# Reading shared rows through several copies in DRAM: roots of a norm in four transfers, rows of decays stored eight times

## The chip, the cores and the metric

The kernel runs on one core of a Trainium2 chip. The metric is the device time of one execution in microseconds. One execution was also taken by the hardware profiler; its page and trace give the start and end of every instruction and DMA. The engines are PE (matmuls; PEld is its weight load), DVE (vector), ACT (scalar, activation functions), POOL (GpSimd) and SP, which here only issues DMAs.

## What is computed

The reference is a state-space layer (Mamba-2 in chunks) with 4 sequences of 8 heads and 768 steps, followed by a feed-forward layer with a gate on its 3072 tokens of width 256:

```python
# batch 4, heads 8, seq 768, head_dim 32, d_state 16
cum = np.cumsum(log_a in the chunk)
L = exp(cum[:, None] - cum[None, :]) * causal          # decays inside a chunk
y = ((C @ B.T) * L) @ x + (C @ state) * exp(cum)       # inside the chunk + from the state
state = exp(sum(la)) * state + sum_j B_j x_j exp(cum_end - cum_j)
...
xn = x / sqrt(mean(x * x) + 1e-6) * rms_g              # x: (3072, 256)
g, val = xn @ w_gate, xn @ w_val                       # 256 -> 1536
out = (g * sigmoid(g) * val) @ w_out                   # 1536 -> 256
```

The inputs of the second layer are float64, so the weights are turned into fp32 on the chip.

## The kernel before, in words

**Blocks.** The tokens are worked on in six blocks of 512. The first layer uses pairs of chunks of 128 steps (a pair is 256 tokens, two pairs make a block). For each block PE makes the products of the first layer (`turn`, `g`, `y`), the sums of squares of the norm (`ms`, L777), the products with w_gate and w_val (`P`, L909) and the products with w_out (`O`, L999). From block 1 on, and for part of block 0, these large products follow a Strassen-Winograd scheme of seven products (`P.1` to `P.7` with sums `C` on DVE, L921; `O.1` to `O.7`). Block 0 also uses plain products (`early` L835, `gate` L825, and the projection `o`, L941), because its weights are not all there yet.

**The order of the work** is written out by hand in one long string, `order`. A step such as `2:P.6.3` names the block, the kind and its numbers. The loop at the end of the kernel calls the functions in that order, and each engine's queue gets its instructions in that order. The tile framework adds the waits between engines. So an engine never overtakes in its own queue, but each queue runs as far ahead of the others as waits allow. In the steps of `kinds`, the steps that prepare a later block carry the number of an earlier one: `1:rb` and `1:xn` belong to block 2, `1:spread` to block 3.

**Weights.** `fetch` (L160) reads one piece of a weight matrix, 256 or 512 KB, into one of four or six buffers. Pieces 0 to 13 alternate between w_gate and w_val in growing columns, pieces 14 to 19 are w_out. DVE takes the mantissa (`man`, L192 and L195), ACT makes the power of two (`pow`, L182 to L185), and DVE multiplies the two (`wt`, L201). `cw` (L879) and `two` (L955) then form the sums of weights for the seven products. All this is done in about the first 95 us.

**The roots.** `rs` makes 1/sqrt on ACT on a 128x128 tile: four groups of 128 tokens, each in 32 equal partitions. It stores them in DRAM as `roots` (4, 32, 128) (L790), and `rb` (`spread_roots`, L794) reads them back so that all 128 partitions hold all 512 roots. `xn` (L802, DVE) multiplies with them.

**The rows of decays.** From the third pair on, the decay matrix L of a group of heads is exp(row - column). `row` makes the sums on PE, `rowout` (`row_store`, L1081) stores them in DRAM as `rowd` (2, 192, 64), and `spread` (L461) reads, for each half of the partitions, one row of 2 KB into 64 partitions. `sub` (L467) subtracts the column, and `ex` (L473) takes the exponential and masks it on POOL. `rowe` and `dT` (L1088, L530) do a similar round trip for the decays exp(cum).

**Queues.** Nearly all DMAs are issued on SP, in the order of the string. The framework gives each DMA one of eight semaphores in turn, so a DMA is issued only when the one eight places earlier has landed, beside its wait for data or a free buffer.

Of the kernel before, what the change touches and what calls it, by code (L numbers as in the profile page):

```python
# [9 lines left out]
FP32 = mybir.dt.float32  # L10
# [10 lines left out]
def kernel(  # L21
# [33 lines left out]
    nc = tc.nc  # L55

    P = 128
    NB, NH, S, D = x.shape
    N = B.shape[-1]
    NC = S // P  # L60
    BH = NB * NH
    NQ = NH // 2
    DM, DF = moe_w_gate.shape
    T = NB * S
# [3 lines left out]
    NT = TB // P  # L68
    NBLK = T // TB
    HC = P // 2  # L70
    halves = [slice(0, HC), slice(HC, P)]
# [101 lines left out]
    parts = {}  # L173
# [31 lines left out]
    warm = const.tile([P, 256], BF16, name="warm")  # L205
# [251 lines left out]
    def spread(g):  # L457
        b, c = divmod(g, NC)
        o = (c * BH + b * NH) * HC
        for u, r in enumerate(halves):  # L460
            nc.sync.dma_start(out=pair_tile(g)[r].rearrange("p h m -> p (h m)"),  # L461
                              in_=rowv[u, o:o + NH * HC].partition_broadcast(HC))
# [329 lines left out]
    def spread_roots(blk):  # L792
        ps["r", blk] = r = nrm.tile([P, TB], FP32, tag="sq2", name="r", bufs=1)
        nc.sync.dma_start(out=r.rearrange("p (t m) -> p t m", t=NT),  # L794
                          in_=roots[blk][:, 0].partition_broadcast(P))
# [281 lines left out]
    def row_store(k):  # L1077
        c = 2 * k
        r_sb = nrm.tile([P, P], FP32, tag="r_sb", name="r_sb", bufs=3)
        nc.vector.tensor_copy(out=r_sb, in_=ps["row", k][:, 0])  # L1080
        nc.sync.dma_start(out=rowd[:, c * BH:(c + 4) * BH].rearrange("u r m -> r u m"),  # L1081
                          in_=r_sb.rearrange("r (u m) -> r u m", u=2))
# [20 lines left out]
    rowd = dram.tile([2, NC * BH, HC], FP32, name="rowd")  # L1103
    rowv = rowd.rearrange("u r m -> u (r m)")
# [58 lines left out]
    def of_chunk(n, fn):  # L1163
# [28 lines left out]
        0:warm 0:a 0:set 0:bc.0 0:bc.1 0:x.0 0:x.1 0:ident 0:fetch.0 0:ones 0:zeros 0:fetch.1 0:mean  # L1192
        0:head 0:upto 0:never 0:after 0:mid 0:upto2 0:gcol 0:mids 0:ident16 0:whole16 0:idle.7
        0:mask.0.0/1 0:whole 0:hmask 0:tmask 0:part 0:part2 0:sel 0:mask.1.1/0 0:fetch.5 0:after2
        0:aT 0:la0 0:kinks 0:mask.0.1/2 0:log4.0.4 0:r.0 0:parts.0 0:eps 0:log 0:d 0:dx 0:c*2 0:cx
        0:log4.4.2 0:log4.6.2 0:scale.0 0:bc.2 0:turn.0.1 0:T.0.1 0:Tt.0.0.1 0:Tt.0.1.1 0:sums.0.1
        0:exp.0.1 0:turn.0.0 0:Tt.0.1.0 0:T.0.0 0:Tt.0.0.0 0:sums.0.0 0:exp.0.0 0:fetch.2 0:turn.1.1
        0:T.1.1 0:Tt.1.0.1 0:Tt.1.1.1 0:scale.1 0:cc 0:g.0.1/2 0:L.0.1 0:turn.1.0 0:Tt.1.1.0
        0:Tt.1.0.0 0:T.1.0 0:sums.1.1 0:exp.1.1 0:A.0 0:S.0 0:A.1 0:S.1 0:man.0 0:g.0.0/1 0:L.0.0
        0:pow.0 0:wt.0 0:man.5 0:pow.1 0:never16 0:last.1 0:Tl.1 0:mask.1.0/2 0:sums.1.0 0:exp.1.0  # L1200
        0:g.1.0/0 0:L.1.0 0:scale.2 0:last.0 0:Tl.0 0:fetch.4 0:fetch.3 0:x.4 0:middles 0:man.1
        0:g.1.1/1 0:L.1.1 0:fetch.6 0:fetch.7 0:pow.5 0:wt.5 0:y.0/2 0:sq.0 0:pow.3 0:row.1
        0:rowout.1 0:rowe.1 0:yt.0 0:ydone.0 0:fetch.12 0:y.1/0 0:r.1 0:row.0 0:man.2 0:fetch.9
        0:fetch.8 0:wt.1 0:early.0.0/1 0:parts.1 0:man.6 0:mask.3/2 0:sums.3 0:pow.2 0:wt.2 0:rowe.0
        0:rowout.0 0:dT.2 1:dT.0 0:sq.1 0:ms.0 0:yt.1 0:ydone.1 0:early.0.1 0:pow.6 0:wt.6
        0:fetch.13 0:man.3 0:exp.3 0:rs.0 0:man.7 0:wt.3 0:turn.2 0:pow.4 0:xn.0 0:mask.2/0 0:sums.2
        0:exp.2 0:early.1.0/2 0:early.1.1 0:man.4 0:wt.4 0:gate.2/0 0:x.2 0:norm.0 0:norm.1 0:T.2
        0:Tt.2.0 0:Tt.2.1 0:Td.2 0:dT.3 0:gg.2/1 1:table 0:silu.0 0:hid.0 0:gate.3/2 0:tx.0 0:man.8
        0:pow.7 0:wt.7 0:L1.2.3 0:L1.2.2 0:man.9 0:silu.2 0:hid.2 0:L.2.0 0:pow.9 0:wt.9 0:A.2 0:S.2
        0:pow.8 0:wt.8 0:silu.3 0:hid.3 0:fetch.11 0:man.11 0:pow.11 0:gate.4/0 0:silu.4 0:hid.4  # L1210
        0:bc.3 0:scale.3 0:fetch.10 0:pow.10 0:man.10 0:cw.3 0:gate.5/1 0:silu.5 0:hid.5 0:x.3
        0:y.2/2 0:pow.12 0:S.3 0:yt.2 0:sq.2 0:ydone.2 0:switch.0 0:P.1.3 0:take.1.3 0:wt.10 0:wt.11
        0:fetch.14 0:switch.1 0:P.2.3 0:man.12 0:turn.3 0:T.3 0:Tt.3.1 0:Tt.3.0 0:Td.3 0:bc.5
        0:P.6.3 0:take.6.3 0:man.13 0:x.5 0:pow.14 0:P.1.4 0:gg.3/2 0:L1.3.2 0:L.3.0 0:L1.3.3 0:bc.4
        0:scale.4 0:P.7.3 0:scale.5 0:y.3/2 0:silu.1 0:C.11.3 0:take.7.3 0:P.5.3 0:P.4.3 0:P.2.4
        0:wt.12 0:pow.13 1:dT.1 0:fetch.18 1:S.0 1:S.1 0:sq.3 0:yt.3 0:ydone.3 0:C.22.3 0:silug.22.3
        0:P.3.3 0:take.1.4 0:silug.21.3 0:ms.1 0:silug.11.3 0:tok 0:fetch.16 0:tokout 0:cw.4 0:P.6.4
        0:C.11.4 0:P.5.4 0:silug.11.4 0:take.6.4 0:P.7.4 1:turn.1 0:wt.13 0:take.7.4 0:C.12.3
        0:silug.12.3 0:P.2.5 0:pow.16 0:man.14 0:hidg.22.3 0:hidg.21.3 0:P.1.5 0:hidg.11.3 0:wt.14
        0:take.1.5 0:o.0/2 1:bc.1 0:hidg.12.3 0:C.22.4 0:P.3.4 0:silug.22.4 0:fetch.15 0:pow.15  # L1220
        0:cw.5 0:P.6.5 0:hid.1 0:o.1 0:C.11.5 0:take.6.5 0:silug.11.5 0:man.15 0:fetch.17 0:fetch.19
        0:P.4.4 0:spread.10 0:C.12.4 0:pow.17 0:silug.12.4 0:silug.21.4 0:wt.15 0:man.17 0:P.5.5
        0:P.7.5 0:take.7.5 0:man.16 0:wt.16 0:pow.18 0:o.2 0:o.3 0:o.4 0:o.5 0:hidg.11.5 0:P.4.5
        0:cw.1 0:C.22.5 0:silug.22.5 1:two.0 0:spread.9 0:exps 0:wt.17 0:spread.8 0:man.18 0:wt.18
        0:rs.1 1:turn.0 0:hidg.11.4 0:hidg.21.4 0:hidg.22.4 1:T.0 1:Tt.0.0 0:silug.21.5 0:hidg.12.4
        0:P.3.5 0:C.12.5 0:man.19 0:pow.19 0:wt.19 0:hidg.21.5 0:silug.12.5 0:hidg.12.5 0:spread.11
        0:sub.11 0:ex.11 0:table.0 0:sub.8 0:o.6 0:o.7 0:o.8 0:o.9 0:o.10 1:T.1 1:Tt.1.0 0:rb.1
        0:xn.1 1:P.1.1 1:take.1.1 1:P.1.0 1:take.1.0 1:P.2.1 1:P.2.0 0:tx.1 1:P.6.1 1:take.6.1
        0:ex.8 0:hidg.22.5 0:o.11 1:P.7.1 0:sub.9 0:ex.9 1:take.7.1 1:bc.0 0:cw.0 1:P.6.0 2:bc.1
        1:C.11.1 1:P.5.1 0:sub.10 0:ex.10 1:x.0 1:cw.2 1:P.4.1 1:take.6.0 1:P.7.0 2:spread.2  # L1230
        1:C.11.0 1:P.5.0 0:table.1 1:C.22.1 1:P.3.1 1:silu.21.1 1:hid.21.1 1:P.1.2 1:C.12.1
        1:silu.11.1 1:hid.11.1 1:silu.22.1 1:hid.22.1 1:take.7.0 1:C.22.0 1:P.4.0 1:take.1.2
        1:silu.11.0 1:hid.11.0 1:silu.21.0 1:hid.21.0 1:silu.12.1 1:hid.12.1 1:two.4 1:P.2.2 1:P.6.2
        1:take.6.2 1:silu.22.0 1:hid.22.0 1:P.1.3 1:take.1.3 1:P.3.0 1:C.12.0 1:s.1 1:P.7.2
        1:take.7.2 1:P.6.3 1:C.11.2 1:take.6.3 1:silu.11.2 1:two.2 1:P.2.3 1:C.11.3 1:P.4.2
        1:silu.21.2 1:P.5.2 1:C.22.2 1:silu.22.2 1:hid.11.2 1:hid.21.2 1:hid.22.2 1:P.7.3 1:take.7.3
        1:P.5.3 1:C.22.3 0:put.0 0:put.1 0:put.3 1:P.3.2 1:C.12.2 1:Tt.0.1 1:Td.0 1:s3.1 1:P.4.3
        1:silu.21.3 1:hid.21.3 1:silu.11.3 1:hid.11.3 1:silu.12.2 1:hid.12.2 1:P.1.4 1:take.1.4
        1:P.3.3 1:C.12.3 1:silu.12.3 1:hid.12.3 0:put.2 1:Tt.1.1 1:Td.1 1:scale2.1 1:silu.22.3
        1:hid.22.3 1:s.3 1:P.1.5 1:take.1.5 1:P.2.5 1:C.11.5 1:silu.12.0 1:hid.12.0 1:P.6.4  # L1240
        1:take.6.4 1:P.2.4 1:C.11.4 1:silu.11.5 1:hid.11.5 1:P.6.5 1:take.6.5 1:P.7.4 1:take.7.4 1:g
        1:L 1:L1.2 1:P.7.5 1:take.7.5 1:L1.3 1:P.5.4 1:C.22.4 1:P.4.4 1:silu.21.4 1:scale2.0 1:P.5.5
        1:C.22.5 1:silu.22.5 1:hid.22.5 1:silu.11.4 1:hid.11.4 1:hid.21.4 1:y.0 1:P.3.4 1:C.12.4
        2:S.0 1:P.4.5 1:silu.21.5 1:hid.21.5 1:s.2 1:P.3.5 1:C.12.5 1:silu.22.4 1:hid.22.4 1:s.0
        1:O.2.0 1:O.2.1 1:silu.12.4 1:hid.12.4 1:s.4 1:s3.4 1:O.1.0 1:O.1.1 1:silu.12.5 1:hid.12.5
        1:O.4.0 1:O.1.2 1:O.1.3 1:x.1 1:y.1 2:S.1 1:sq 1:spread.0 1:yt 1:O.1.4 1:O.1.5 1:Otake.1
        1:s.5 1:exps 1:spread.2 1:s3.3 2:dT.0 1:O.4.1 1:O.4.2 1:O.5.0 1:s2.0 1:O.5.1 1:s2.1 1:O.5.2
        1:s2.2 1:O.5.3 1:O.5.4 1:s2.4 1:s2.3 1:O.5.5 1:s2.5 1:s3.2 1:s3.0 1:sub.2 1:ms 1:rs 1:O.6.0
        1:s4.0 1:O.6.1 1:O.6.2 1:s4.1 1:O.6.3 1:O.6.4 1:O.6.5 1:Otake.6 1:s4.3 1:s4.4 2:turn.0 2:T.0
        2:Tt.0.1 1:rb 1:s4.5 1:s4.2 1:s3.5 2:dT.1 2:turn.1 2:T.1 2:Tt.1.0 2:Tt.1.1 2:Tt.0.0 2:Td.0  # L1250
# [138 lines left out]
```

## Time and profile before

| what | value |
|---|---|
| median of 3 runs | 407.25 us (405.87 to 407.42) |
| the profiled execution | 406.08 us, of which the span is 404.3 us |
| PE busy | 395.5 us (98%) |
| DVE busy | 296.5 us (73%) |
| ACT busy | 223.9 us (55%) |
| DMA moved | 26.99 MB, mean 67 GB/s |
| HBM read / written | 22.64 MB / 3.74 MB |

Busy times are sums over the whole span, which has stages with different limits: a first stage of about 67 us in which weights are converted and PE does many small products, five blocks of large products, and a short tail for the last outputs. The windows of the profile give busy time, clock, DMA share and GB/s for each stretch; the chain of waits gives what released what.

### The profile page before, as it was taken

The page shows a single profiled execution, that of the slowest core. Times are in us where ns is not written, and L with a number is a line of the kernel's source. Part 1 is how long each engine was busy: PE and PEld are TensorE (multiplying, and loading weights), DVE is VectorE, ACT ScalarE, POOL GpSimd, SP SyncE. Part 2 cuts the span into 40 slices and gives each one's busy share as a digit, 9 for nine tenths or more (in the row PEclk, how much of TensorE's full clock was granted, in tenths as well). Part 3 has the DMA queues.
Part 4 walks back from the last instruction along what each step waited for, and adds up shares of the span by engine and source line. Part 5 has one row for each costly group of instructions (what it writes and reads, how often), then busy time and mean ns, then how long its engine had stood idle before and what let it go on. Part 6 is the DMA issues. An engine that isn't in the chain of part 4 may idle for free.

```text
span 404.3 us, 9559 instructions
## 1 busy us (share of the span) xinstructions
PE 395.5 (98%) x3881; PEld 338.6 (84%) x3881; DVE 296.5 (73%) x686; ACT 223.9 (55%) x456; POOL 37.6 (9%) x57
## 2 busy tenths in 40 slices
PE   8989999999999998999999999999999999999997
PEld 5656467888888898988899888899988899988896
DVE  6999999987687885567786566877657666475772
ACT  3989986967756343744552654372674461445410
POOL 2210000002300011400011300011400010000000
PEclk9999999999999999999999999999999999999999
DMA  9988968427001126600414210303000003100001
GB/s 112 203 248 222 219 89 230 129 44 93 27 0 54 29 73 103 67 0 4 106 51 115 46 34 0 69 8 92 1 2 2 2 2 87 52 0 2 0 2 52
DMA packets 92355, 26.99 MB, mean 67 GB/s; under 512 B 77048, under 2 KB 86136, under 8 KB 92312
## 3 DMA queue, kind: packets, MB, share of 16 engines
q1 hardware_dynamic: 88152, 26.13, 30.8%
q10 hardware_dynamic: 4160, 0.26, 0.8%
q8 instruction: 30, 0.49, 0.5%
q14 instruction: 13, 0.11, 0.1%
HBM read 22.64 MB, written 3.74 MB: 65 GB/s over the span
## 4 chain that ended last, share of the span: by engine, by line
PE 85%; DVE 6%; DMA 4%; ACT 2%; issue 1%; SPq 1%; DVEq 0%; ACTq 0%
PE gate L909 28%; PE val L909 21%; PE o L999 17%; PE o L941 5%; PE gate L825 3%; PE y L699 3%; DMA r<-roots 2%; DMA dT<-rowe 2%; PE gate L835 1%; PE g L562 1%; PE y L627 1%; PE e L426 1%; DVE m L195 1%; DVE wgv L201 1%; DVE xn L802 1%
## 5 line engine op out<-in xcount | busy, mean ns | idle before, releaser
L921 DVE TENSOR_TENSOR c<-val,p 128x512 f32<-128x512 f32 x99 | 67.8, 689 | 35.1 <-PE val L909 30.9
L915 ACT COPY p<-gate 128x512 f32<-128x512 f32 x99 | 57.4, 581 | 51.9 <-PE gate L909 47.6
L909 PE MATMUL gate<-tx,sw 128*128 128x256 f32 x264 | 65.6, 382 | 0.0
L930 ACT ACTIVATE c<-c 128x256 f32<-128x256 f32 x99 | 39.7, 415 | 44.2 <-DVE c L921 44.1
L909 PEld LDWEIGHTS gate<-tx,sw 128*128 128x128 f32 x264 | 49.3, 190 | 7.4 <-ACT p L915 0.5
L934 DVE TENSOR_TENSOR h<-c 128x256 f32<-128x256 f32 x99 | 40.4, 420 | 11.4 <-ACT c L930 10.9
L909 PE MATMUL gate<-xn,wgv 128*128 128x256 f32 x132 | 33.4, 383 | 1.4 <-DVE xn L802 1.3
L909 PE MATMUL val<-xn,sw 128*128 128x256 f32 x132 | 33.7, 381 | 0.8 <-DVE c L921 0.8
L909 PE MATMUL val<-tx,sw 128*128 128x256 f32 x132 | 33.4, 381 | 0.0
L909 PE MATMUL val<-xn,wgv 128*128 128x256 f32 x132 | 33.2, 380 | 0.0
L909 PE MATMUL gate<-tx,wgv 128*128 128x256 f32 x132 | 32.8, 380 | 0.0
L475 POOL TENSOR_SCALAR_AFFINE_SELECT L<-L 64x512 f32<-64x512 f32 x32 | 23.6, 738 | 92.1 <-ACT L L473 90.6
L999 PE MATMUL o<-wo,h 128*128 128x128 f32 x240 | 30.3, 277 | 0.0
L999 PEld LDWEIGHTS o<-wo,h 128*128 128x128 f32 x240 | 28.7, 192 | 0.9 <-issue 0.4
L909 PEld LDWEIGHTS gate<-xn,wgv 128*128 128x128 f32 x132 | 24.3, 190 | 5.3 <-issue 1.6
L999 PE MATMUL o<-two,s 128*128 128x128 f32 x240 | 28.7, 275 | 0.0
L909 PEld LDWEIGHTS val<-xn,sw 128*128 128x128 f32 x132 | 24.7, 190 | 4.5 <-DVE c L921 1.2
L999 PE MATMUL o<-two,h 128*128 128x128 f32 x240 | 28.4, 275 | 0.0
L999 PEld LDWEIGHTS o<-two,s 128*128 128x128 f32 x240 | 27.8, 192 | 0.3 <-issue 0.2
L909 PEld LDWEIGHTS val<-tx,sw 128*128 128x128 f32 x132 | 24.8, 190 | 3.4
L909 PEld LDWEIGHTS gate<-tx,wgv 128*128 128x128 f32 x132 | 24.8, 190 | 3.3
L999 PEld LDWEIGHTS o<-two,h 128*128 128x128 f32 x240 | 27.6, 192 | 0.0
(188 smaller groups left out, 612.3 us busy)
## 6 DMA issues: line engine op xcount, KB each, us to landing
L<-rowd SPq DMA_DIRECT2D x32, 128.0 KB, 5.9
xr<-in_x_dram SPq DMA_DIRECT2D x24, 128.0 KB, 4.3
wr<-in_moe_w_out_dram SPq DMA_DIRECT2D x6, 512.0 KB
wr<-in_moe_w_val_dram SPq DMA_DIRECT2D x5, 512.0 KB, 7.1
wr<-in_moe_w_gate_dram SPq DMA_DIRECT2D x5, 512.0 KB, 6.6
out_dram<-ob SPq DMA_DIRECT2D x9, 256.0 KB, 2.6
br<-in_B_dram SPq DMA_DIRECT2D x22, 64.0 KB, 4.2
cr<-in_C_dram SPq DMA_DIRECT2D x22, 64.0 KB, 3.3
```

Source lines behind the costliest of these rows:

```text
L195: nc.vector.scalar_tensor_tensor(out=f, in0=lo.bitcast(U32), scalar=2.0 ** -32, in1=m, op0=ALU.mult, op1=ALU.add)
L201: nc.vector.scalar_tensor_tensor(out=dst, in0=f, scalar=2.0 ** -20, in1=e, op0=ALU.mult, op1=ALU.mult)
L475: nc.gpsimd.affine_select(out=L[r], in_=L[r], pattern=[[0, NH], [1, HC]], compare_op=ALU.is_ge, fill=0.0, base=0, channel_multiplier=-1)
L699: nc.tensor.matmul(out=y[2 * k + u][rows, (2 * n + i) * HC:(2 * n + i + 1) * HC], start=(k, u, rows.start) not in opened, stop=True, skip_ ...
L825: nc.tensor.matmul(out=gv[:, k], lhsT=w[:, t, fs], rhs=xns[0][:, t], start=(t == 0), stop=(t == 1))
L909: nc.tensor.matmul(out=dst[:, half[w]], lhsT=lhsT, rhs=rhs, start=(k in (1, 2, 5) and w == 0), stop=True, skip_group_check=True)
L915: nc.scalar.copy(out=t, in_=Xs[j])
L921: nc.vector.tensor_tensor(out=t, in0=Zs[j], in1=a, op=ALU.add)
L930: nc.scalar.activation(out=u, in_=src[:, half[0]], func=AF.Silu)
L934: nc.vector.tensor_tensor(out=hidden_tile(blk, j)[:, c // 10 - 1, c % 10 - 1], in0=u, in1=src[:, half[1]], op=ALU.mult)
L941: nc.tensor.matmul(out=o, lhsT=hs_[blk, f // 2][:, f % 2, k // 2, (k % 2) * P:(k % 2 + 1) * P], rhs=wo[:, f], start=opens, stop=(f == NF - ...
L999: nc.tensor.matmul(out=o[t] if apart else o[:, t * P:(t + 1) * P], lhsT=lhsT[:, t], rhs=rhs, start=(k in (1, 2, 4, 5) and j == 0 and (apar ...
```

## The change

Three DMA patterns change. The roots are read back by four transfers of 32 partitions, and partition q of each group reads copy q of the 32 that are in DRAM. The rows of decays are stored eight times: two transfers in place of one, each writing eight copies in pieces of 64 numbers (256 bytes). The readers of a row take copy 0 to 7, eight partitions each. With this, the string `order` is another one throughout: the same 1548 steps, in another sequence, and with other choices among the three pairs of PSUM banks in the first stage (the number behind a slash).

```diff
     def spread(g):
         ...
             nc.sync.dma_start(out=pair_tile(g)[r].rearrange("p h m -> p (h m)"),
-                              in_=rowv[u, o:o + NH * HC].partition_broadcast(HC))
+                              in_=rowv[:, u, o:o + NH * HC].unsqueeze(1).to_broadcast(
+                                  [8, HC // 8, NH * HC]))
...
     def spread_roots(blk):
         ps["r", blk] = r = nrm.tile([P, TB], FP32, tag="sq2", name="r", bufs=1)
-        nc.sync.dma_start(out=r.rearrange("p (t m) -> p t m", t=NT),
-                          in_=roots[blk][:, 0].partition_broadcast(P))
+        for k in range(P // 32):
+            nc.sync.dma_start(
+                out=r[32 * k:32 * k + 32].rearrange("p (t m) -> p t m", t=NT),
+                in_=roots[blk].rearrange("t q m -> q t m"))
...
         nc.vector.tensor_copy(out=r_sb, in_=ps["row", k][:, 0])
-        nc.sync.dma_start(out=rowd[:, c * BH:(c + 4) * BH].rearrange("u r m -> r u m"),
-                          in_=r_sb.rearrange("r (u m) -> r u m", u=2))
+        for u, r in enumerate(halves):
+            nc.sync.dma_start(out=rowd[:, u, c * BH:(c + 4) * BH].rearrange("k r m -> r k m"),
+                              in_=r_sb[:, r].unsqueeze(1).to_broadcast([P, 8, HC]))
...
-    rowd = dram.tile([2, NC * BH, HC], FP32, name="rowd")
-    rowv = rowd.rearrange("u r m -> u (r m)")
+    rowd = dram.tile([8, 2, NC * BH, HC], FP32, name="rowd")
+    rowv = rowd.rearrange("k u r m -> k u (r m)")
```

Of the string, the part of the first stage from the second row store's old place to the first Winograd products. Before:

```
0:rowout.1 0:rowe.1 0:yt.0 0:ydone.0 0:fetch.12 0:y.1/0 0:r.1 0:row.0 0:man.2 0:fetch.9
0:fetch.8 0:wt.1 0:early.0.0/1 0:parts.1 0:man.6 0:mask.3/2 0:sums.3 0:pow.2 0:wt.2 0:rowe.0
0:rowout.0 0:dT.2 1:dT.0 0:sq.1 0:ms.0 0:yt.1 0:ydone.1 0:early.0.1 0:pow.6 0:wt.6
0:fetch.13 0:man.3 0:exp.3 0:rs.0 0:man.7 0:wt.3 0:turn.2 0:pow.4 0:xn.0 0:mask.2/0 0:sums.2
...
0:pow.8 0:wt.8 0:silu.3 0:hid.3 0:fetch.11 0:man.11 0:pow.11 0:gate.4/0 0:silu.4 0:hid.4
0:bc.3 0:scale.3 0:fetch.10 0:pow.10 0:man.10 0:cw.3 0:gate.5/1 0:silu.5 0:hid.5 0:x.3
0:y.2/2 0:pow.12 0:S.3 0:yt.2 0:sq.2 0:ydone.2 0:switch.0 0:P.1.3 0:take.1.3 0:wt.10 0:wt.11
```

After:

```
0:fetch.12 0:row.1 0:pow.3 0:rowout.1 0:yt.0 0:ydone.0 0:rowe.1 0:y.1/2 0:r.1 0:fetch.13
0:row.0 0:man.2 0:fetch.9 0:wt.1 0:early.0.0/0 0:parts.1 0:man.6 0:mask.3/1 0:sums.3 0:pow.2
0:wt.2 0:rowe.0 0:dT.2 0:sq.1 0:ms.0 0:yt.1 0:ydone.1 0:early.0.1 0:man.3 0:wt.3 0:mask.2/2
0:sums.2 0:pow.6 0:fetch.8 0:wt.6 0:man.4 0:x.2 0:exp.3 0:early.1.0/1 0:rs.0 0:norm.0 0:xn.0
0:pow.4 0:wt.4 0:fetch.10 0:man.7 0:dT.3 0:turn.2 0:early.1.1 0:norm.1 0:rowout.0 0:exp.2
...
0:fetch.14 0:wt.7 0:tx.0 0:gg.2/1 0:L1.2.2 0:L1.2.3 0:L.2.0 0:man.8 0:gate.3/2 0:pow.9
0:fetch.11 0:silu.2 0:hid.2 0:pow.8 0:wt.9 0:wt.8 0:man.11 0:silu.3 0:hid.3 0:A.2 0:S.2
```

In SP's queue this makes 17 more DMAs: 15 for the roots and 2 for the rows. On ACT one more load of a table of functions stands in the order.

## The prediction

> **What bounds the kernel now.** I read the page's busy table first, then the slices, then PE by stage, the chain of waits, and last the DMA issues.
>
> ```profile
> PE 395.5 (98%) x3881; PEld 338.6 (84%) x3881; DVE 296.5 (73%) x686; ACT 223.9 (55%) x456; POOL 37.6 (9%) x57
> ...
> PEclk9999999999999999999999999999999999999999
> DMA  9988968427001126600414210303000003100001
> ```
>
> PE is busy for 98% of the span at the full granted clock. Since the change leaves the set of matmuls alone, only PE's idle 8.8 us can be won. The DMA row shows one crowded stretch, the first quarter. The windows say where the idle time lies:
>
> ```profile
> 20.00:30.00 10.00, 8.67 (x114) 5.45 (x111) 9.72 (x23) 8.60 (x17) 1.50 (x2) 1.00 0.91 250
> 30.00:40.00 10.00, 10.00 (x96) 6.55 (x102) 9.76 (x21) 9.18 (x15) 0.00 (x0) 1.00 0.82 225
> 40.00:50.00 10.00, 10.00 (x70) 4.43 (x55) 9.79 (x22) 9.10 (x14) 0.00 (x0) 1.00 1.10 226
> ...
> 52.00:67.00 15.00, 13.62 (x321) 10.27 (x321) 14.14 (x38) 13.57 (x33) 1.73 (x2) 1.00 0.76 135
> ...
> 67.00:400.00 333.00, 331.56 (x3067) 298.64 (x3064) 234.57 (x524) 169.24 (x353) 29.40 (x36) 1.00 0.20 43
> ```
>
> The columns are length, then PE, PEld, DVE, ACT, POOL busy, clock, DMA share, GB/s. From 67 to 400 us PE idles 333.00 - 331.56 = 1.44 us; from 52 to 67 us 1.38 us, behind a DVE busy 14.1 of 15. The rest lies in the first 52 us and the tail (about 3.1 and 2.9 us). From 20 to 50 us DMA is busy 28.3 of 30 us, and DVE, which turns the 64-bit weights into fp32, 29.3 of 30. The chain of waits names the one gap after 67 us:
>
> ```profile
> 149.90 1.54 DMA roots<-r
> 151.52 8.38 DMA r<-roots
> 160.82 1.96 PE gate L909 x8
> ```
>
> The roots of block 2 are stored and read back through DRAM, xn follows on DVE, and PE's first product waits 1.27 us at 160.8. That read is slow for its size, and so is the read of the rows:
>
> ```profile
> L<-rowd SPq DMA_DIRECT2D x32, 128.0 KB, 5.9
> ...
> r<-roots SPq DMA_DIRECT2D x5, 256.0 KB, 8.2
> ...
> roots<-r SPq DMA_DIRECT2D x5, 64.0 KB, 1.5
> ...
> rowd<-r_sb SPq DMA_DIRECT2D x2, 64.0 KB, 5.3
> ```
>
> **The change, part by part.** The sum is made against the profiled execution: 406.08 us, of which 404.3 are the span and 1.8 lie around it. It is 1.17 us under the median of 407.25 and inside the spread of those runs (405.87 to 407.42), so I add 1.17 at the end. About 0.5%, 2.0 us, is what a measurement can tell from no change.
>
> *Roots in four transfers.* All 128 partitions read the same four rows of 512 bytes; from 335.4 to 341.8 us, with little else moving, the windows give 69 GB/s, while outputs at 351 us moved at 308. Now 32 partitions read 32 stored copies, four times. Bounds for the new read: four issues at 0.37 to 0.6 us apiece and a 64 KB landing of 1.5 us, so 3.0 to 3.9 us (estimate); at worst, if only the volume counts, the old 8.2. I take 3.5, since the roots' store is the nearest row (64 KB, the same pieces). What it is worth depends on the order. Between the sums ms of block 2 and its first product the old order holds 11.1 us of other PE work, the new one 13.3 (products L999 at 0.111 us apiece, L909 at 0.216, counted in the two orders). The chain ms 0.4, roots 0.7, store 1.6, read, xn 1.5, with 0.4 of hand-overs, is 4.6 plus the read: 8.1 with 3.5, 12.8 with the old 8.2. Both fit under 13.3, so the 1.27 us go by the new order alone; the faster read is insurance. At the other boundaries 12.4 to 18.6 us stand between, and nothing waited there; for block 1 the order shows 6.1 us, but ACT reaches those roots 3 us of work earlier than before, and PE has some 19 us to do after its sums. Gain: **-1.4** (between 0 and -1.44). xn's waits on DVE (5.7 us in 3) vanish too; past 67 us DVE idles 30%, so that is worth nothing by itself, and if that cover were gone it would cost up to 3.1 at one boundary. SP issues 15 more transfers, 15 x 0.5 = 7.5 us over the span; its queue mostly waits for ACT and DVE, so 0.
>
> *Rows stored eight times.* Each of the two stores becomes two transfers, 512 KB in 2,048 pieces of 256 bytes instead of 64 KB in 256. The readers gain little: L's reads are issued long before their use, and DVE never waits for one; 0. The stores fall into the crowded stretch. No row shows such pieces alone. Nearest is the page's queue table: q1's 88,152 packets took 30.8% of 16 x 404.3 us, 22.6 ns for 296 bytes on average; q10's 4,160 of 64 bytes took 0.8%, 12.4 ns. About 20 ns for 256 bytes, divided over 16 engines, is 2.6 us per store, **+2.2 us** more than the old one (estimate). The Trainium skill speaks against this edit: "DMA: Bandwidth & Descriptors", the table of properties at its head, says that pieces under 512 bytes are read, modified and written. If that moves the bytes twice, 1 MB at the 273 GB/s of 22.8 to 33.8 us takes 3.8 us, +3.4 per store. Writing could also be absorbed for half the price (+1). I take 2.2, which rests on packets of this trace, and keep 1 to 3.4; the skill's value would add 2.4 us to the lateness below.
>
> *The order, rewritten in all queues.* The instructions are the same, except 17 more DMAs and one more table load on ACT. That load (1.28 us, L1142) comes at 70 to 80 us, where ACT is busy 16.4 of 20; cover 3.6, cost 0. POOL, 9% busy, keeps its sequence. Through the first 60 us of DVE work nearly every landmark (the products L601, the weights L201, S) stands within 2 us of its old place, most at it, and the new order is a little kinder: from the start of y.2, P.3.3 of column pair 3 has 11.7 us of PE work ahead in both orders, while C.22.3, which it waits for on DVE, ends after 12.7 us of DVE work before and 11.1 after (0.6 us for 512 elements, 0.35 for 256, start to start). The worst pair of this kind was 1.0 short and is now level. With punctual weights that would close about 1.1 of the 1.38 us.
>
> But the weights come later on SP's queue. Old order: first row store, pieces 12, 9, 8, second row store, 13, x.2, 11, 10, 14. New: 12, first row store, 13, 9, 8, x.2, 10, second row store, 14, then 11. Piece 11 gets 10 and 14 ahead of it (512 KB at 273 GB/s is 1.9 us each, at the 353 of 30 to 32 us 1.5: 3.0 to 3.8) and two dearer stores (4.4), less the free DMA time of 30 to 40 us (1.8): 5.6 to 6.4 later. It was issued at 38.60; at 4 us of transfer that is 42.6, so now 48.2 to 49.0. Its mantissa on DVE (man.11, L192 at 47.47 before) is moved forward in DVE's order by 2.0 us of work, to about 45.4. Late by about 3 us. Queued behind man.11 on DVE are hid.3, S.2, hid.4, the sums sw, hid.5, and PE's first Winograd products wait for the banks which hid.4 and hid.5 free. There DVE had 0.4 us of idle before S.3 and 0.26 at the first C, and PE keeps up to 1 us in hand at y.2: roughly 1.0 is absorbed, 2.0 arrives. Idle from 52 to 67 us: 1.38 - 1.1 + 2.0 = 2.3, that is **+0.9**. Piece 9 lands near 36 to 37 us and is wanted at 37 to 38: cover about 1 us, cost 0 unless the stores run slower.
>
> *Start and tail.* The first 20 us and the last transfers keep their contents; of the last two half stores one now leaves some 0.5 us later, still 2.7 us of matmuls before the end. 0, with 0.3 either way.
>
> Sum: -1.4 + 0.9 = -0.5 on 406.08, 405.6; on the median's scale 406.7. Because the two sides of the lateness are uneven (none at all is possible), I state 406.5.
>
> **The rivals.**
>
> *Punctual weights, 0.30.* Slices of 350 GB/s and more occur (30 to 32 and 68 to 70 us), and no DVE row waits for a weight now. Then -1.44 - 1.1 = -2.5: 404.7; at best, with another 1 us from the first 52 us, 403.4. Against it: DMA has no more than 2 us free from 20 to 50 us and about 4.4 more to carry.
>
> *The stores hold up the weights, 0.30, slower.* The place is SP's queue between 24 and 46 us, the mechanism the 4,096 small pieces ahead of pieces 13, 9, 14 and 11, the price what DVE waits at man.9 and man.11. At the skill's price man.11 is 5.4 late, piece 9 adds about 1, and some 5 reach PE: -1.4 - 1.1 + 5 = +2.5, 409.8. If the stores ran at the 69 GB/s of the crowded reads, 512 KB would take 7.6 us each and the time 412 or more. It decides from about 4.5 us of delay at DVE: 4.5 - 1.4 - 1.1 = +2.0.
>
> *The change does not do what it says.* If a row read is limited by something other than sharing, r still lands after 8 us, which the order covers: the same 406.5. No separate chance.
>
> **How the numbers follow.** The main case has 0.40, 405.0 to 408.5 by itself, nearly all within 0.5% (405.2 to 409.3). Punctual weights: 0.28 faster, 0.02 same. Held weights: 0.28 slower, 0.02 same. With 0.04 of the main case faster and 0.02 slower: faster 0.32, same 0.38, slower 0.30. Range 403.2 to 411.2: from the best case to a store at somewhat more than the skill's price, leaving out 1 in 10 at either end.
>
> **What would show it.** Right: r<-roots landing in 3 to 4 us, no PE wait near 160 us, PE at 332 or more of the 333 us after the first stretch, a DVE wait of 1 to 4 us at L192 for a weight transfer near 46 us, and PE idle 1.5 to 3 us in the next 20. Wrong: no DVE wait for wr at all (then the rival of punctual weights), waits over 4.5 us there, or new PE gaps over 1 us beyond 70 us, where I expect none.

## The result, and the profile after

The changed kernel takes 405.66 us (median of 20 runs, 403.98 to 407.68), the kernel before 407.26 us (20 runs, 405.69 to 408.11): a ratio of 0.997, 95% interval 0.9956 to 0.9984. A second series gave 0.9971 (0.9955 to 0.9986). So the change gains 0.3%, which is inside the 0.5% that the forecast counted as no change, and lies within its range. What the medians hide is that two chances in the first 30 us, neither of them part of the change, move each execution by about as much. They are separated below.

The profiled execution of the changed kernel took 406.05 us, with a span of 404.0. Its busy table and DMA slices:

```profile
PE 397.3 (98%) x3881; PEld 340.1 (84%) x3881; DVE 297.9 (74%) x686; ACT 224.4 (56%) x456; POOL 37.2 (9%) x57
...
DMA  9899989209012214400223700203000001100001
```

PE shows 1.8 us more busy time for the same 3881 matmuls, which is a first sign that they did not all run at the same speed. The windows, in the stretches of the prediction (length; PE, PEld, DVE, ACT, POOL busy; clock, DMA share, GB/s):

```profile
20.00:30.00 10.00, 8.97 (x148) 5.75 (x146) 9.75 (x22) 9.10 (x19) 1.68 (x2) 1.00 0.92 276
30.00:40.00 10.00, 9.60 (x73) 6.63 (x73) 9.80 (x20) 9.81 (x16) 0.00 (x0) 1.00 0.95 252
40.00:50.00 10.00, 10.00 (x77) 4.40 (x76) 8.96 (x19) 7.21 (x12) 0.00 (x0) 1.00 1.05 260
...
52.00:67.00 15.00, 13.78 (x343) 10.03 (x341) 14.14 (x36) 12.53 (x25) 0.74 (x1) 1.00 0.88 186
67.00:400.00 333.00, 332.89 (x3077) 299.65 (x3078) 238.51 (x533) 172.68 (x362) 29.79 (x37) 1.00 0.19 42
```

From 67 to 400 us PE now idles 0.11 us instead of 1.44. From 52 to 67 us it idles 1.22 instead of 1.38, nearly as before. The chain of waits around block 2, where it had run through the store and the read of the roots, now stays on PE:

```profile
149.71 0.36 PE ms L778 x8
150.06 1.09 PE o L1002 x8
...
153.81 8.04 PE o L1002 x72
161.85 1.73 PE gate L912 x8
```

The sums ms end at 150.1 us, and at 161.9 the first product starts with no DMA between. In the trace's DMA records (start, length and size of each packet) the 512 packets of one read of roots took 1.9 to 2.2 us (120 to 135 GB/s); before they took 5.2 to 6.9 us (38 to 50 GB/s). Nothing waits for roots any more. The page of this profile gives no landing times; what is seen in its DMA issues is the number and size of the transfers:

```profile
r<-roots SPq DMA_DIRECT2D x20, 64.0 KB
rowd<-r_sb SPq DMA_DIRECT2D x4, 256.0 KB
```

What waits now is this (engine, line, what it waited for: us in total, times, longest):

```profile
ACT e L182 <- DMA wr<-in_moe_w_val_dram: 2.0, 2, 1.4
...
DVE m L192 <- DMA wr<-in_moe_w_val_dram: 0.9, 1, 0.9
```

DVE waits once, 0.9 us, for weight piece 11, which landed at 48.4 us: the place that the prediction named, and its landing time too (the latter by luck, as the second profile shows), with a shorter wait. Of ACT's two waits 1.4 us is for the same piece.

### The profile page after: what moved, and what is told of

It reads as the page before. It is cut to its first block, busy times and chain, and to the rows that moved or that the text cites. A ratio compares the mean times of both kernels' runs of the same rounds, so it can differ in the third digit from the quotient of the medians.

```text
span 404.0 us, 9594 instructions
## 1 busy us (share of the span) xinstructions
PE 397.3 (98%) x3881; PEld 340.1 (84%) x3881; DVE 297.9 (74%) x686; ACT 224.4 (56%) x456; POOL 37.2 (9%) x57
## 3 DMA queue, kind: packets, MB, share of 16 engines
HBM read 22.64 MB, written 4.65 MB: 68 GB/s over the span
## 4 chain that ended last, share of the span: by engine, by line
PE 84%; ACT 4%; DVE 4%; DMA 3%; SPq 3%; issue 1%; DVEq 0%
PE gate L912 28%; PE o L1002 23%; PE val L912 21%; PE o L944 5%; PE y L700 3%; DMA wr<-in_moe_w_val_dram 3%; SPq L121 2%; PE g L563 1%; ACT e L182 1%; ACT e L183 1%; PE tp L506 1%; SPq L128 1%; ACT e L185 1%; DMA br<-in_B_dram 1%; SPq L160 1%
## 5 line engine op out<-in xcount | busy, mean ns | idle before, releaser
L912 PEld LDWEIGHTS val<-xn,wgv 128*128 128x128 f32 x132 | 24.8, 190 | 3.5 <-issue 0.2
```

The costliest lines, as they stand in the source:

```text
L912: nc.tensor.matmul(out=dst[:, half[w]], lhsT=lhsT, rhs=rhs, start=(k in (1, 2, 5) and w == 0), stop=True, skip_group_check=True)
```

## The experiments

All twelve were timed in five rounds, each next to the kernel before on the same chip: e1 to e4 on one chip, e5 to e8 on a second, e9 to e12 on a third. The kernel before took 406.83, 406.6 and 406.09 us there, so medians compare best within a group. The idle time of PE by stage explains them better than the medians do, so here it is first, from the windows of each profile (us; "clock" is when the matmuls went from half to full rate, read from their start times):

| kernel | profiled us | span | clock | idle 20-30 | idle 52-69 | idle 69-398 |
|---|---|---|---|---|---|---|
| before | 406.08 | 404.3 | 5.3 | 1.33 | 1.38 | 1.44 |
| changed | 406.05 | 404.0 | 10.4 | 1.03 | 1.27 | 0.06 |
| changed again (e1) | 404.92 | 403.2 | 5.4 | 1.98 | 1.41 | 0.00 |
| new order, old transfers (e2) | 404.08 | 402.3 | 4.5 | 1.94 | 0.76 | 0.00 |
| changed, rows once (e3) | 404.39 | 402.4 | 3.9 | 2.41 | 0.77 | 0.00 |
| old order, new transfers (e4) | 405.80 | 404.0 | 10.4 | 1.38 | 1.38 | 0.00 |
| changed, piece 11 earlier (e5) | 405.41 | 403.4 | 10.3 | 1.37 | 0.78 | 0.00 |
| e2, e_sb ahead of piece 3 (e6) | 404.03 | 402.2 | 5.3 | 1.74 | 0.77 | 0.00 |
| e6, start filled (e7) | 404.36 | 402.5 | 6.6 | 1.74 | 0.76 | 0.00 |
| old order, four roots (e8) | 405.77 | 404.0 | 10.1 | 1.37 | 1.37 | 0.00 |
| before, start filled (e9) | 407.08 | 405.3 | 4.5 | 2.24 | 1.36 | 1.65 |
| changed, start filled (e10) | 403.17 | 401.3 | 3.9 | 1.09 | 0.77 | 0.00 |
| old order, four roots, filled (e11) | 404.50 | 402.7 | 6.5 | 1.38 | 1.39 | 0.00 |
| new order, rows once, filled (e12) | 404.19 | 402.1 | 6.2 | 1.73 | 0.76 | 0.00 |

### The changed kernel again

No edit. 

> The changed kernel once more, for a second profile. In the first one PE ran at half its rate from 5.2 to 10.3 us (the 192-column products L379 start 0.32 us apart, before 0.16), under a granted clock of 1.00. Theory A: this is the warm-up of PE's clock, whose moment falls by chance in every execution, of both kernels. Then a second execution can have it or not; if not, L379 stands at 0.16 us, the start comes some 1.5 to 1.8 us sooner, DVE waits 2 to 3 us for weight piece 11 at L192 instead of 0.9, and PE's idle time from 50 to 67 us is 2 to 3 us. Theory B: it belongs to the new order of the start; then 0.32 us again, tp L512 again at 10.6. Both: time 0.997 of the kernel before, PE at least 332.5 of 333 us from 67 to 400 us.

Measured: 405.12 us (404.53 to 407.08, 12 runs), ratio 0.9971 (0.9955 to 0.9986). The timeline of PE shows what differed between the two profiles (start, length, engine, line, operation). The first profile of the changed kernel:

```profile
7.09 0.85 PE L379 MATMUL d_ps<-la,upto 128*128 128x192 f32 x2
7.73 0.85 PE L379 MATMUL d_ps<-la,after 128*128 128x192 f32 x2
```

The second:

```profile
6.60 0.49 PE L379 MATMUL d_ps<-la,upto 128*128 128x192 f32 x2
6.93 0.49 PE L379 MATMUL d_ps<-la,after 128*128 128x192 f32 x2
```

The same pair of matmuls takes 0.64 us from one row to the next in the first and 0.33 in the second. Theory A holds: the half rate is not part of the change, and the granted clock of the page (1.00 in both) does not show it. The clock cost 0.8 us of span (404.0 to 403.2), not the expected 1.5 to 1.8, because a stage behind it gave some of the time back: in the second profile PE idles 1.98 us from 20 to 30 us instead of 1.03. DVE's wait for piece 11 is 1.0 us and not 2 to 3, a miss of the same term as in the prediction:

```profile
47.41 0.43 DVE L192 TENSOR_SCALAR m<-wr 128x512 int32<-128x512 int32 x1 [1.02 <-DMA wr<-in_moe_w_val_dram]
```

In brackets stand the idle time before the row and what ended it. From 67 to 400 us PE is busy 332.93 of 333, and the stage that the next runs are compared with is:

```profile
52.00:67.00 15.00, 13.65 (x345) 10.54 (x346) 14.14 (x37) 12.53 (x27) 0.74 (x1) 1.00 0.85 185
```

### The new order with the old transfers

```diff
-        for k in range(P // 32):
-            nc.sync.dma_start(
-                out=r[32 * k:32 * k + 32].rearrange("p (t m) -> p t m", t=NT),
-                in_=roots[blk].rearrange("t q m -> q t m"))
+        nc.sync.dma_start(out=r.rearrange("p (t m) -> p t m", t=NT),
+                          in_=roots[blk][:, 0].partition_broadcast(P))
...
-        for u, r in enumerate(halves):
-            nc.sync.dma_start(out=rowd[:, u, c * BH:(c + 4) * BH].rearrange("k r m -> r k m"),
-                              in_=r_sb[:, r].unsqueeze(1).to_broadcast([P, 8, HC]))
+        nc.sync.dma_start(out=rowd[:, c * BH:(c + 4) * BH].rearrange("u r m -> r u m"),
+                          in_=r_sb.rearrange("r (u m) -> r u m", u=2))
```

The shape of `rowd` and its reader are those of before as well.

> The new order with both DMA patterns of before: one read of the roots, rows stored once. Theory A (the new order alone closes the gap at block 2, the faster read is insurance; the dearer stores only delay weights): r<-roots lands after about 8 us, yet no PE wait at 150 to 165 us, PE at least 332.5 of 333 us from 67 to 400; DVE's wait at L192 for a weight under 0.5 us; time 0.5 to 1.0 us under the changed kernel. Theory B (the four transfers close the gap): a PE wait of 0.5 to 1.5 us near 160 us for xn is back, and the time is 0.5 to 1.5 us over the changed kernel.

Measured: 404.12 us (403.69 to 405.46, 6 runs), ratio 0.9942 (0.9924 to 0.996). Its windows:

```profile
52.00:67.00 15.00, 14.31 (x340) 11.07 (x332) 13.89 (x35) 12.73 (x27) 1.02 (x1) 1.00 0.88 214
```

and its waits for roots and weights:

```profile
DVE xn L802 <- DMA r<-roots: 2.2, 3, 0.8
ACT e L182 <- DMA wr<-in_moe_w_val_dram: 1.9, 1, 1.9
```

DVE still waits for the slow read at three boundaries (0.8 us at most), but PE idles 0.00 us from 69 to 398 us: the order alone closes the gap. It does so narrowly. At block 2:

```profile
158.91 1.42 DVE L802 SCALAR_TENSOR_TENSOR xn<-yt,gcol,r 128x512 f32<-128x512 f32 x2 [0.84 <-DMA r<-roots]
...
159.81 1.97 PE L909 MATMUL gate<-xn,wgv 128*128 128x256 f32 x8
```

The first of the two xn takes 0.75 us and ends at 159.66, some 0.2 us before PE wants it. DVE no longer waits for piece 11 (0.4 us for another piece, at 26.7 us, is left; ACT's 1.9 us is piece 3, at 23 us), and from 52 to 67 us PE is busy 14.31 of 15 us instead of 13.65. Theory A, with 1.0 us under the changed kernel at the upper end of what it expected.

### The changed kernel with rows stored once

The second hunk of the diff above, with the shape of `rowd` and its reader:

```diff
-    rowd = dram.tile([8, 2, NC * BH, HC], FP32, name="rowd")
+    rowd = dram.tile([2, NC * BH, HC], FP32, name="rowd")
```

> The changed kernel with the rows of decays stored once, as before; the roots still in four transfers. Theory A (the eightfold stores cost through the weights that come later): piece 11 lands 2 to 4 us sooner than at 48.4 us, DVE's wait at L192 and ACT's at L182 for weights (0.9 and 2.0 us) are gone or under 0.5 us, and the time falls by 0.5 to 1.0 us. Theory B (the place of piece 11 in the queue alone makes it late, the stores are free): waits and time stay within 0.3 us. Theory C (the eight copies help the readers): L waits longer for rowd somewhere and the time rises.

Measured: 404.56 us (403.57 to 405.24, 6 runs), ratio 0.9948 (0.9929 to 0.9966). Piece 11 is there before DVE wants it at 46.2 us, and idle time from 52 to 69 us falls from 1.41 (second profile of the changed kernel) to 0.77. This is theory A, 0.64 us in that stage:

```profile
52.00:67.00 15.00, 14.30 (x348) 11.20 (x340) 13.89 (x34) 12.86 (x27) 1.01 (x1) 1.00 0.85 209
```

Theory C falls: a read of the rows lands 3.2 us after its issue here. In the DMA records a 2 KB packet past 95 us takes a median of 84 ns with eight copies and with one, and the reads as a whole are slower with eight (figures below, under the rows).

### The old order with both new transfers

The kernel before with both edits of transfers in full; its string `order` stays. Of the edit:

```diff
-    rowd = dram.tile([2, NC * BH, HC], FP32, name="rowd")
+    rowd = dram.tile([8, 2, NC * BH, HC], FP32, name="rowd")
```

> The old order with both new DMA patterns. Theory A (a read of 3 to 4 us in place of 8.4 also closes the gap, since the old order holds 11.1 us of PE work there; the old place of piece 11 in the queue makes the stores' price invisible): no PE wait near 160 us, PE about 332.8 of 333 us from 67 to 400, no wait for weights over 0.5 us, time 1.0 to 1.4 us under the kernel before, as good as the changed kernel. Theory B (only the order closes it): the wait near 160 us stays at 1 us or more and the time is that of the kernel before. Theory C (the stores cost by themselves): new waits for weights of 1 us or more between 30 and 50 us, and a time no better than before in spite of the gap.

Measured: 405.86 us (405.33 to 410.02, 12 runs), ratio 0.9994 (0.9972 to 1.0017), which is inconclusive: three times (407.2, 409.3 and 410.0 us) pull the ratio up, and what made them stays open. The profile is clear on the mechanism:

```profile
67.00:400.00 333.00, 332.70 (x3077) 299.74 (x3078) 236.54 (x529) 170.97 (x358) 29.79 (x37) 1.00 0.19 44
```

From 69 to 398 us PE idles 0.00: the faster read alone closes the gap too. No engine waits for a weight transfer at all, and the idle time from 52 to 69 us is 1.38 us, as in the kernel before. So in the old order the stores load the DMA engines without delaying anything that the profile shows; what they cost in the new order comes through the place of piece 11. This holds for an execution with a late clock, which this profile is.

### Weight piece 11 ahead of piece 10

```diff
-        0:pow.4 0:wt.4 0:fetch.10 0:man.7 0:dT.3 0:turn.2 0:early.1.1 0:norm.1 0:rowout.0 0:exp.2
+        0:pow.4 0:wt.4 0:fetch.11 0:man.7 0:dT.3 0:turn.2 0:early.1.1 0:norm.1 0:rowout.0 0:exp.2
...
-        0:fetch.11 0:silu.2 0:hid.2 0:pow.8 0:wt.9 0:wt.8 0:man.11 0:silu.3 0:hid.3 0:A.2 0:S.2
+        0:fetch.10 0:silu.2 0:hid.2 0:pow.8 0:wt.9 0:wt.8 0:man.11 0:silu.3 0:hid.3 0:A.2 0:S.2
```

> The changed kernel, both new transfers kept, with the reads of weight pieces 11 and 10 exchanged in the queue, so that 11 is issued near 36 us, ahead of the second row store, and 10, which is wanted 5 us later, near 43. Theory A (the eightfold stores cost only because piece 11 stands behind them): DVE's wait at L192 (1.0 us in the second profile of the changed kernel) and ACT's second wait at L182 go, PE gets from 13.65 to about 14.3 of 15 us between 52 and 67 us, and the time falls by 0.5 to 0.7 us, to about 404.5. Theory B (the stores load the DMA engines and whatever stands behind them is late): the wait moves to piece 10 or 14 at the same length, time within 0.3 us of the changed kernel.

Measured: 404.92 us (403.44 to 406.77, 12 runs), ratio 0.9952 (0.9934 to 0.9971). The profiled execution has the late clock, so it is compared with the first profile of the changed kernel:

```profile
40.00:50.00 10.00, 10.00 (x77) 4.50 (x76) 9.82 (x24) 7.92 (x13) 0.00 (x0) 1.00 1.05 257
...
52.00:67.00 15.00, 14.29 (x346) 10.84 (x345) 13.87 (x35) 12.32 (x26) 1.01 (x1) 1.00 0.95 201
```

DVE is busy 9.82 us of 40 to 50 us instead of 8.96, no weight is waited for, PE gets 14.29 of 15 us instead of 13.78, and the span is 403.4 instead of 404.0. With both new transfers kept, two words exchanged in the string give back the 0.6 us: theory A. The medians differ by only 0.2 us, less than two chances of the start make.

### The exponentials ahead of piece 3

```diff
-        0:fetch.12 0:row.1 0:pow.3 0:rowout.1 0:yt.0 0:ydone.0 0:rowe.1 0:y.1/2
+        0:fetch.12 0:row.1 0:rowout.1 0:rowe.1 0:pow.3 0:yt.0 0:ydone.0 0:y.1/2
```

> The new order with the old transfers (the kernel of 404.1 us), with one step moved: ACT takes the exponentials e_sb of row group 1 (rowe.1) before it turns to weight piece 3, not after. PE waited 1.2 us at 23.5 us for that e_sb, and ACT had waited 1.95 us for piece 3 ahead of it (before the change PE's wait was 0.4 us). Theory A: that wait of PE goes, PE is busy 8.8 us or more of the 10 from 20 to 30 us (8.06 now), and up to 1 us of it reaches the end: 403.2 to 403.8. Theory B (DVE sets the pace from 20 to 50 us, PE only waits later instead): PE's idle time moves to 25 to 35 or 52 to 67 us, and the time stays within 0.3 us of 404.1.

Measured: 403.84 us (403.59 to 404.14, 6 runs), ratio 0.9935 (0.9918 to 0.9952). PE's wait for e_sb, behind piece 3, is gone, and another takes its place:

```profile
28.27 1.13 PE L773 MATMUL ms<-sq,mean 128*128 128x512 f32 x2 [0.96 <-POOL sq L741]
```

From 20 to 30 us PE idles 1.74 us instead of 1.94, and the median is 0.28 us lower: theory B. What did change is the spread, 0.55 us where the kernel without this edit has 1.8.

### The start filled

```diff
-        ... 0:after2 0:aT 0:kinks 0:la0 0:mask.0.1/1 0:log4.0.4 0:fetch.5 0:r.0 ...
+        ... 0:after2 0:aT*1 0:kinks 0:la0 0:idle.1 0:mask.0.1/1 0:log4.0.4 0:fetch.5 0:r.0*1 ...
```

> The kernel of the run before, with three matmuls on dummy data put into PE's short idle times at the start (one before the transposes aT near 4.3 us, one before the second mask near 5.1, one before r_ps near 6.0). Theory A (PE's clock doubles at the end of a busy stretch[...], whose place is chance, and the idle times of 4 to 6 us make a stretch fail): no execution has the half rate after about 7 us, L379 stands at 0.16 us, and the spread of the times is under 1.5 us where that of the kernel before is 2; median 0 to 0.7 us lower. Theory B (the idle times have nothing to do with it): the spread stays, the three matmuls cost up to 0.3 us.

Measured: 404.24 us (404.14 to 404.54, 6 runs), ratio 0.9945 (0.9929 to 0.9962). The spread is 0.40 us, but that of the run before was as small, so the times do not decide. The profile does: this execution's clock rose at 6.6 us.

```profile
7.11 0.49 PE L379 MATMUL d_ps<-la,upto 128*128 128x192 f32 x2
7.44 0.49 PE L379 MATMUL d_ps<-la,after 128*128 128x192 f32 x2
```

In the nine profiles without filling the clock rises either by 5.4 us (five) or after 10.0 (four). All five filled kernels have the full rate by 6.7 us, and three of them get it between 6.2 and 6.6 us, where none of the nine does. The Trainium skill has this rule, in "TensorE: Matmul & The Clock Gate", Part 1: PE's clock is halved until one window of about 3.4 us was busy, and the windows run freely against the kernel's start. The profiles fit it: with the page's 3.4 us, 10.1 to 10.4 us is one window after 6.7 to 7.0 (an estimate), so by this reading a window that ended there did not count as busy in four profiles because of the idle times of 4 to 6 us, and the next one decided. That it is those idle times is shown only by the filled kernels; how much idle time a window may hold, no run here shows. The three matmuls cost 0.3 us of span (402.2 to 402.5), as theory B had it.

### The old order with four transfers of roots

```diff
-        nc.sync.dma_start(out=r.rearrange("p (t m) -> p t m", t=NT),
-                          in_=roots[blk][:, 0].partition_broadcast(P))
+        for k in range(P // 32):
+            nc.sync.dma_start(
+                out=r[32 * k:32 * k + 32].rearrange("p (t m) -> p t m", t=NT),
+                in_=roots[blk].rearrange("t q m -> q t m"))
```

> The old order with the roots in four transfers and the rows stored once: the smallest edit that could close the gap at block 2. Theory A (the read alone is enough): no PE wait at 150 to 165 us, PE about 332.8 of 333 from 67 to 400 us, no wait for weights over 0.3 us, time 1.0 to 1.4 us under the kernel before, about 405.6. Theory B (the eightfold stores helped the old order, which had 405.9 with them): 0.5 us or more above that. If the stores cost the old order something that its profile did not show, it is 0.5 us or more below 405.9, and the times over 407 of that kernel don't occur.

Measured: 404.5 us (404.03 to 405.92, 12 runs), ratio 0.9963 (0.9948 to 0.9979). PE idles 0.00 us from 69 to 398 us, so this one edit does what the whole change does there. Its page has landing times for both kinds of read (operation, count, size, us from issue to landing):

```profile
L<-rowd SPq DMA_DIRECT2D x32, 128.0 KB, 3.4
...
r<-roots SPq DMA_DIRECT2D x20, 64.0 KB, 2.0
```

The rows land after 3.4 us instead of 5.9 with a single copy stored, so the eight copies are not needed for that (the new order alone, e2, has 3.9).

Its times form two groups, 404.0 to 404.7 and 405.4 to 405.9; the profile, with the late clock, is of the upper one. Against the old order with the stores (405.86) it looks 1.4 us better, yet both profiles have a late clock, a span of 404.0 us and the same idle times. How often each drew the early clock could make the difference, but that is not shown: seven of twelve times are in the lower group here and none of twelve in e4, and one execution of each was profiled. That the stores cost the old order something when the clock comes early stays open; the old order with the stores and a filled start was not run.

### Four kernels with the start filled

The three matmuls of the filled start were added to four kernels, to take one of the two chances out. The four are: the kernel before; the changed kernel; the old order with four transfers of roots; and the new order with four transfers of roots, rows stored once and `rowe.1` ahead of `pow.3`. The edit in the old string, as an example:

```diff
-        0:aT 0:la0 0:kinks 0:mask.0.1/2 0:log4.0.4 0:r.0 ...
+        0:aT*1 0:la0 0:kinks 0:idle.1 0:mask.0.1/2 0:log4.0.4 0:r.0*1 ...
```

Before: 

> The kernel before, with the three dummy matmuls at the start and nothing else. Its times fall into two groups, 405.3 to 406.4 and 406.6 to 408.1 us. Theory A (the groups are the executions whose PE clock doubles near 5 us and near 10 us): with the idle times filled the second group is gone, all times lie within 1 us, at the first group plus 0.1 to 0.4 us for the three matmuls: 405.9 to 406.7; the profile has L379 at 0.16 us. Theory B (something else makes the groups): they stay, 1.2 to 1.6 us apart.

Measured: 406.45 us (405.63 to 407.28, 12 runs), ratio 1.0001 (0.9985 to 1.0017). No time is over 407.3 any more, but two groups remain (405.6 to 406.2 and 406.7 to 407.3). The profile is of the upper group although its clock rose at 4.5 us, so the clock cannot be the only cause. It shows a second candidate: PE waits 1.29 us for e_sb, and ACT, which makes it, had waited for weight piece 3:

```profile
25.33 0.49 PE L1074 MATMUL r_ps<-mids,la 128*128 128x128 f32 x2 [1.29 <-ACT e_sb L1087]
```
```profile
23.50 0.53 ACT L182 ACTIVATE e<-wr,kinks 128x256 int16<-128x256 int16 x1 [2.08 <-DMA wr<-in_moe_w_val_dram]
```

In the profile of the kernel before, the same row of PE had waited 0.39 us, with piece 3 there 0.8 us sooner. The idle time from 20 to 30 us is 0.91 us longer than in that profile, and the span 1.0 us. That this wait parts the two groups is likely by this one pair of profiles, not shown. A long wait here is not a matter of the order, as I had taken it to be after the second profile of the changed kernel.

Changed: 

> The changed kernel with the same three matmuls. Theory A: no time over 406 us any more (it had up to 407.7), all within 1 us, 404.8 to 405.6; against the filled kernel before this is the change without the chance of the clock, and should be -1.1 us, as between the two profiles with an early clock (spans 404.3 and 403.2). Theory B (the change is worth what the medians say): -1.6 us. Theory C (the prediction's sum): -0.5 us.

Measured: 404.06 us (403.17 to 404.42, 6 runs), ratio 0.9939 (0.9915 to 0.9963). That is 2.4 us under the filled kernel before, more than any theory had. The profile is the fastest of all, 403.17 us:

```profile
20.00:30.00 10.00, 8.91 (x112) 5.60 (x112) 9.72 (x23) 8.95 (x17) 1.50 (x2) 1.00 1.04 286
...
52.00:67.00 15.00, 14.23 (x286) 10.80 (x275) 14.27 (x38) 12.52 (x28) 1.13 (x1) 1.00 0.93 218
```
```profile
DVE m L192 <- DMA wr<-in_moe_w_val_dram: 0.6, 1, 0.6
```

Piece 3 came early (PE idles 1.09 us from 20 to 30 us), and DVE's wait for piece 11 was 0.6 us instead of 1.0, of which nothing reached PE: 14.23 of 15 us. Against the second profile of the changed kernel (403.2) the span is 1.9 us shorter: 0.9 is idle time from 20 to 30 us, 0.6 from 52 to 69 us, 0.4 is PE's busy time. Only the last can be put down to the earlier clock (3.9 us against 5.4) by what the runs show. Why piece 3 came early here, and why the filled start lowered the median of this kernel (ratio to the kernel before 0.9939, unfilled 0.9971) and not that of the kernel before (1.0001), stays open.

Old order, four roots: 

> The old order with four transfers of roots, rows stored once, and the three matmuls. Theory A (the reads of the roots close the gap of 1.27 us by themselves): 1.2 to 1.5 us under the filled kernel before, about 404.6 to 405.2, so as good as the whole change or better. Theory B (half of the 2.2 us that it was ahead of the kernel before came from the chance of the clock, and the stores are harmless in the old order): within 0.3 us of the filled changed kernel.

Measured: 404.17 us (403.68 to 404.75, 7 runs), ratio 0.9945 (0.9924 to 0.9966), 2.3 us under the filled kernel before and level with the filled changed kernel. Both theories had a part of it; the size is larger than both gave.

New order, rows once: 

> What the runs point to as the best of the parts: the new order, four transfers of roots, rows stored once, the exponentials e_sb of row group 1 ahead of weight piece 3, and the three matmuls. Theory A (each saves what its own run showed): 0.7 to 1.0 us under the filled changed kernel, 403.9 to 404.4 us, all within 0.8 us, PE 14.2 of 15 us from 52 to 67 us. Theory B (the eightfold stores cost nothing once the clock is even): within 0.3 us of the filled changed kernel.

Measured: 404.13 us (404.06 to 404.52, 7 runs), ratio 0.9942 (0.992 to 0.9964), level with the filled changed kernel: theory B. What the stores cost in two profiles of the changed kernel (0.5 us against e5, 0.64 against e3) was absent in the third, and in these medians it cannot be seen.

Several kernels beat both: e2, e6, e10, e11 and e12, at 403.8 to 404.2 us, 0.2 to 0.5% under the changed kernel's 405.1 and 405.7. Among themselves these runs do not tell them apart. The simplest of them leaves both DMA patterns as they were.

## Why the prediction was right, and where it was not

**The sum.** Between the two profiles with an early clock the span falls from 404.3 to 403.2 us: -1.1, where the prediction had -0.5. The terms, from the table and the busy times of both pages: idle time after 69 us -1.44, from 52 to 69 us +0.03, from 20 to 30 us +0.65, PE's busy time -0.2 and the tail -0.1. The forecast of 406.5 us is 0.8 over the median; the medians fell by 1.6 us, twice the 0.75 that it implied. That the sum is not further off is partly luck: order and lateness were put at +0.9 us together and came to 0.0, while the start, put at 0, cost 0.65 in this pair.

**The roots, -1.4.** Right in size and in its main reason. It measured -1.44, the new order alone gives it (e2), and the faster read was insurance. But the cover was counted too long: from the end of the sums to the first product the new order has 11.8 us of PE work (13.3 in the prediction), the old one 10.5 (11.1). With the slow read the gap closes all the same, by 0.2 us, because the first product waits for the first of the two xn only (0.75 us, where the chain had 1.5 for both). What the prediction left unsaid, though its own numbers gave it (a chain of 8.1 us against 11.1 in the old order), is that the read alone suffices as well (e4, e8, e11). The two halves of the change buy the same 1.4 us. The read was put at 3.5 us; the 2.0 to 2.4 us that the pages of e3, e8, e11 and e12 show for each of the four transfers, which overlap, and 2 us for all packets, are better than that. The 69 GB/s read for the old one held 0.18 MB of other transfers; its own 512 packets ran at 40.

**The rows.** The two eightfold stores took 3.35 and 3.32 us in the DMA records of the changed kernel (3.18 and 3.05 in its second profile), and the single ones 1.3 and 2.5 before: +2.0 and +0.8 us, where 2.2 was taken for each. A packet of 256 bytes took 18 ns (20 was estimated). The Trainium skill's rule, in "DMA: Bandwidth & Descriptors", Specifications, that pieces under 512 bytes are read, modified and written, from which the prediction estimated +3.4 us, did not show as a doubling: 512 KB passed at 157 to 172 GB/s beside weight transfers, HBM read stayed at 22.64 MB, and HBM written rose from 3.74 to 4.65 MB, which is only what is stored more.

The readers gained nothing, as predicted; they even lost. Past 95 us the same 1,536 packets of 2 KB were under way for 26.4 to 28.4 us in all in the five kernels with eight copies, and for 21.2 to 23.5 us in the nine with one. At most 11 or 12 packets were under way at once with eight copies, 18 to 20 with one. That the smaller number is what slowed them is a reading of these records; no run tests it. PE did not pay for it: from 69 us on it idles 0.06 us or less in these kernels. In the changed kernel only POOL (9% busy) waited for a row, 6.2 us, once.

**The order, -1.1 with punctual weights.** Mis-sized: the six kernels in which the new order had its weights in time (e2, e3, e5, e6, e7, e12) idle 0.76 to 0.78 us from 52 to 69 us against 1.36 to 1.39 in every old order, so -0.6.

**The late piece 11, +2.0.** This is the step that failed most. DVE was to be there at 45.4 us and would have waited 3. Even undisturbed (e2) it is there only at 46.1; in the second profile of the changed kernel, whose clock came as early as in the profile that the sum was made on, it waited from 46.4 to 47.4. So the piece landed at 47.3 us there, 0.9 to 1.7 sooner than predicted (48.2 to 49.0). The 48.4 us of the first profile agree by luck: with its late clock DVE, too, is 1.1 us later. So 1.0 us arrived at DVE and some 0.65 at PE, and at 0.6 us of wait nothing did (e10). The prediction's absorption of about 1 us was too high, and its wait three times too long; the net of order and lateness was 0.0, not +0.9.

**Start and tail, 0 with 0.3 either way.** Wrong as a bound for one execution: the clock moves PE's busy time by 2.0 us (395.3 and 397.3 in the two profiles of the changed kernel), and the idle time from 20 to 30 us, where the wait behind piece 3 lies, goes from 1.09 to 2.41 us in the profiles without a late clock. Both were seen in either order, so they need not spoil a forecast of medians, but the clock is the reason why the profiled executions of before and after, at 406.08 and 406.05 us, look alike.

**The rivals.** Punctual weights were put at 404.7 us: this is about what the kernels of the new order show whose weights do come in time (403.8 to 404.9 us), so the mechanism was right and needed one more edit. The stores as the brake needed 4.5 us of delay at DVE; 1.0 came. That the read of the roots would land after 8 us as before is out: its four transfers land in 2.0 to 2.4 us each, side by side. The extra table load of ACT and the 17 more DMAs left no wait that the profile shows; the load's cover was misread, though (16.4 us are of 60 to 80 us; from 70 to 80 ACT was busy 9.37 of 10).

## What to carry to other kernels

Where a gap is closed twice, by giving the engine other work and by making the transfer faster, undo each by itself: one of the two is often free to go, with what it costs elsewhere. When a transfer gets dearer, look at what stands behind it in its queue and is wanted first; exchanging two entries left as little idle time in that stage here (0.78 us) as taking the transfer away (0.77). When copies are made so that readers do not share, look at how many packets are under way at once as well: here the copies lowered it. And before reading a difference of 1 us between two profiles, look at how fast equal matmuls ran in each and how long the same early transfer took.

## What the runs showed of the hardware

PE can run at half its rate for the first 4 to 10.4 us under a granted clock of 1.00 on the page; only the start times of equal matmuls tell (0.32 against 0.16 us for 192 columns). Four of nine profiles with an unfilled start had it until after 10 us, none of five with a filled one. Between the two profiles of the changed kernel it is worth 2.0 us of PE's busy time and about 0.8 us at the end.

Reading the same four DRAM rows from 128 partitions in one transfer ran at 38 to 50 GB/s in the kernel before; reading 32 copies, one for each of 32 partitions, in four transfers, ran at 107 to 141. In the profiles of before and after, packets of 512 bytes took a median of 25 to 27 ns in both, but the longest of a read took 0.1 to 1.2 us in the first and 0.2 to 0.35 us in the second, and on average 2.7 to 6.3 packets of a read were under way against 6.9 to 7.8. Whether the copies or the four transfers at once made the difference stays open: no run has one without the other.

A row of 2 KB read by 64 partitions gained nothing from eight copies: the same packets were under way for about a quarter longer in all, with at most 12 at once instead of 18 to 20.
